# Sums of w_in moved to block 6, and another order of products, silus and sums in the last two blocks of a fused linear attention and MoE kernel

## Chip, cores and metric

The kernel runs on one core of one Trainium2 chip. The metric is the device time of one execution in microseconds (us), given as the median over runs of the same program; a profiled execution, one of its own, is where all views of the profile come from. TensorE is called PE here, VectorE DVE, ScalarE ACT, GpSimd POOL and SyncE SP, as in the profile.

## What is computed

The inputs are q, k and v of shape 8 x 8 x 576 x 64 (batch, heads, positions, head width), w_in (512 x 2048), w_out (2048 x 512) and beta (2048), all f32. The reference is a linear attention and then a layer with a gated activation:

```python
q_p, k_p = phi(q), phi(k)                      # elu(x) + 1
kv  = np.einsum('bhsd,bhse->bhde', k_p, v)
num = np.einsum('bhsd,bhde->bhse', q_p, kv)
den = np.einsum('bhsd,bhd->bhs', q_p, k_p.sum(2))[..., None] + 1e-06
x = (num / den).transpose(0, 2, 1, 3).reshape(4608, 512)
h = x @ w_in
g = h / (1 + np.exp(-beta * h))
return g @ w_out
```

## The kernel before

**Blocks.** The work goes by nine blocks of 512 tokens. Block b (0 to 7) holds 512 of the 576 positions of batch b; the 64 that are left over of each batch are gathered in a buffer `xT_tail` and make up block 8. Block 0 is written out by hand ahead of the loop; the loop `for b in range(1, B + 1)` (L1019, B = 8) does blocks 1 to 8. A block has two phases. In the first, H, PE computes h = x w_in, 16 tiles of 128 features by 512 tokens, and ACT writes silu(beta h) to SBUF as bf16 (`silu`, L409; w_out has been divided by beta before, which makes up for the factor). In the second, Y, PE computes g w_out, DVE and ACT add the parts, and SP stores the result.

**The order** of the work is written out by hand: each engine's queue runs in the order in which the program issues it, and an instruction that waits holds up those behind it on its engine. The attention of the following batches is put between as side work: `at(side, n, f)` says that f is issued at place n of a phase, `run(side, n)` issues it. In block 6 the H phase issues at place 1 the products k^T v of batch 7 (`kv_both`, evicted by DVE at L230 into `kv_q`), and at place 4 its numerators (`numer_all`: matmuls L332, DVE evictions L345 to L347, transposing DMAs L354).

**Fast products in Y.** `y_fast` does, in blocks 1 to 8, a 2 x 2 block product with 7 products in place of 8 (Strassen's in Winograd's form). It halves the tokens (columns 0:256 and 256:512 of g), the features (tiles 0 to 7 and 8 to 15) and the columns of w_out. It needs sums of w_out's blocks (`ws`, made once) and of g's blocks (`gs`, four buffers in `stage`, made by DVE in every block): `g_diff` (L723) makes gs[2]; `g_sums` (L730, L731) gs[0] and gs[1]; `g_last` (L726) gs[3] from gs[1]. Each is made in two calls of four tiles. The order on PE is ya (g plain), yd (gs[2]), ya again, yc (gs[1]), yb (gs[0]), yd again, yb again (gs[3]), 16 matmuls of 256 columns each (L951). Between them ACT copies ya (L967, L972) and DVE adds (L975 u2, L976 u3, L985, L988, L996). Block 8's yb goes in three parts (L923, L931), so that the last store is small.

**Fast products in H.** Blocks 1 to 6 use `h_phase`: sixteen plain tiles one after another. Blocks 7 and 8 use `h_fast`: eight tiles plain (4 to 7 and 12 to 15; `h_mm`, four matmuls of 512 columns, L401), and two groups of four (0 to 3 and 8 to 11) by the 2 x 2 scheme with 7 products of four matmuls of 256 columns each (`product`, L833). For this DVE makes sums of w_in (`h_w_sums(0)` and `h_w_sums(2)`, four subtractions or additions each, L785 to L788), which serve both blocks and lie in the buffer of v's f32 copy (`vf`, from which POOL's casts, L240, made `vaug`), and sums of x (`h_x_sums`, L807).

`products(fq)` gives the parts of one group. They use two two-bank PSUM tiles, `cw` (halves cw0 and cw1; the profile's `hc`) and `z` (one bank used; `hz`), and one bank z6 (also `hz`):

- `part1`: z6; DVE copies it to h_u[0] (L845). Then cw0 and z. DVE adds cw0 into h_u[0] (L852), and z and h_u[0] into h_u[1] (L853).
- `part2`: a product into cw1, one on top of cw0; DVE adds cw1 and h_u[1] into half of c2 (L858).
- `part3`: one product on top of z, one on top of cw1; DVE adds z and h_u[0] into the other half of c2 (L863) and h_u[0] into cw1 (L864).
- `out(0)`: two silus from cw. `out(1)`: two silus from c2 (L871).

The dependences are kept per tile, so the product into cw1 also waits for the addition L852, which reads cw0. PSUM banks come from a pool of four single banks (plain tiles, z6, ya to yb) and one of two double banks (cw and z).

Of the kernel before, what the change touches and what calls it, by code (L numbers as in the profile page):

```python
# [16 lines left out]
def kernel(  # L17
# [10 lines left out]
    nc = tc.nc  # L28

    B, H, S, D = q.shape  # L30
# [9 lines left out]
    HM = DM // 2  # L40
# [16 lines left out]
    def banks(name, shape=None, dt=F32):  # L57
# [13 lines left out]
    g_sb = [consts.tile([P, FC, 512], BF16, name=f"g{i}") for i in range(2)]  # L71
# [20 lines left out]
    gs = [  # L92
        st_b[:, n * 2048 : (n + 1) * 2048].rearrange("p (c t) -> p c t", c=8) for n in range(4)
    ]
# [189 lines left out]
    def rows_of(t):  # L284
        return P if t < NT - 1 else G
# [273 lines left out]
    for t in range(NT):  # L559
        n = rows_of(t)  # L560
# [157 lines left out]
    def at(side, n, *fs):  # L718
        side.setdefault(n, []).extend(fs)

    def g_diff(b, c):
        g = g_sb[b % 2]
        nc.vector.tensor_sub(gs[2][:, c], g[:, c, 0:HM], g[:, c, HM:512])  # L723

    def g_last(b, c):
        nc.vector.tensor_sub(gs[3][:, c], g_sb[b % 2][:, 8 + c.start : 8 + c.stop, 0:HM], gs[1][:, c])  # L726

    def g_sums(b, c0, c1, last=True):
        g, c, c2 = g_sb[b % 2], slice(c0, c1), slice(8 + c0, 8 + c1)
        nc.vector.tensor_add(gs[0][:, c], g[:, c, HM:512], g[:, c2, HM:512])  # L730
        nc.vector.tensor_sub(gs[1][:, c], gs[0][:, c], g[:, c, 0:HM])  # L731
        if last:
            g_last(b, c)

    def g_parts(b, ff):
        if ff in (3, 7):
# [4 lines left out]
    def h_phase(b, x, side):  # L741
# [31 lines left out]
    h_u = [  # L773
        xk[1].rearrange("p i j d -> p (i j d)").bitcast(F32)[:, n * 512 : (n + 1) * 512]
        for n in range(2)
    ]

    def h_w_plain(fq, f, r):

        return w_in_sb[fq][:, 2 * r : 2 * r + 2, f * 256 : (f + 1) * 256]  # L780

    def h_w_sums(fq):

        s, a = h_ws[fq // 2], lambda f, r: h_w_plain(fq, f, r)
        nc.vector.tensor_add(s[0], a(1, 0), a(1, 1))  # L785
        nc.vector.tensor_sub(s[1], s[0], a(0, 0))
        nc.vector.tensor_sub(s[2], a(0, 0), a(1, 0))
        nc.vector.tensor_sub(s[3], a(0, 1), s[1])  # L788

    def h_x_plain(b, r, t):  # L790

        if b == B:
            return xT_tail[:, :, 4 * t : 4 * t + 4, r]
        return xT[b % 2][:, :, 4 * t + r : 4 * t + 4 : 2]

    def h_x_sums(b):

        t = h_xs[b % 2]
        x = lambda r, t: h_x_plain(b, r, t)

        def like(a, c):
            return a.rearrange("p i (t n) -> p i t n", n=c.shape[-1])

        for k, (u, w) in enumerate((
            (x(0, 1), x(0, 0)), (x(1, 1), t[0]), (x(1, 1), x(0, 1)), (x(1, 0), t[1])
        )):
            nc.vector.tensor_sub(like(t[k], u), u, like(w, u) if k % 2 else w)  # L807

    def h_fast(b, x, side):
        run(side, 0)  # L810
        hps_of = {}

        def plain(ff):
            hps_of[ff] = bank("h_ps")
            h_mm(x, ff, hps_of[ff])

        def act(*ffs):
            for ff in ffs:
                silu(b, ff, hps_of[ff])

        def products(fq):
            s, t = h_ws[fq // 2], h_xs[b % 2]
            cw, z = banks("hc"), banks("hz")[:, 0]
            c2 = h_c2

            def product(ps, lhs, rhs, first):
                for a in range(2):
                    for i in range(2):
                        o = ps[:, a * 256 : (a + 1) * 256]
                        m = rhs[:, i]  # L830
                        if len(m.shape) > 2:
                            o = o.rearrange("p (t n) -> p t n", n=m.shape[-1])
                        nc.tensor.matmul(  # L833
                            o, lhs[:, i, a * P : (a + 1) * P], m,
                            start=(first and a == 0 and i == 0), stop=True,
                            skip_group_check=True,
                        )

            def w(f, r):
                return h_w_plain(fq, f, r)  # L840

            def part1():
                z6 = bank("hz")
                product(z6, s[1], t[1], True)
                nc.vector.tensor_copy(h_u[0], z6)  # L845

                for n in (1, 0) if fq == 0 else (0, 1):
                    if n:
                        product(cw[:, 0], w(0, 0), h_x_plain(b, 0, 0), True)
                    else:  # L850
                        product(z, s[2], t[2], True)
                nc.vector.tensor_add(h_u[0], cw[:, 0], h_u[0])  # L852
                nc.vector.tensor_add(h_u[1], z, h_u[0])  # L853

            def part2():
                product(cw[:, 1], s[0], t[0], True)
                product(cw[:, 0], w(0, 1), h_x_plain(b, 1, 0), False)
                nc.vector.tensor_add(c2[:, 1], cw[:, 1], h_u[1])  # L858

            def part3():  # L860
                product(z, w(1, 1), t[3], False)
                product(cw[:, 1], s[3], h_x_plain(b, 1, 1), False)
                nc.vector.tensor_add(c2[:, 0], z, h_u[0])  # L863
                nc.vector.tensor_add(cw[:, 1], cw[:, 1], h_u[0])  # L864

            def out(n):

                for a in range(2):
                    ff = 4 * fq + 2 * n + a
                    src = (cw, c2)[n][:, :, a * 256 : (a + 1) * 256]  # L870
                    nc.scalar.activation(  # L871
                        g_sb[b % 2][:, ff].rearrange("p (t n) -> p t n", t=2), src,
                        ACTF.Silu, scale=beta_c[:, ff : ff + 1],
                    )

            return part1, part2, part3, out

        p1, p2, p3, out = products(0)
        p1()
        plain(4)  # L880
        act(4)
        p2()
        plain(5)
        act(5)
        p3()
        plain(6)
        act(6)
        out(0)
        plain(7)
        act(7)  # L890
        out(1)
        plain(12)
        act(12)
        p1, p2, p3, out = products(2)
        p1()
        g_diff(b, slice(0, 4))
        plain(13)
        act(13)
        p2()
        plain(14)  # L900
        act(14)
        p3()
        out(1)
        g_diff(b, slice(4, 8))
        plain(15)
        act(15)
        out(0)
        g_sums(b, 4, 8)
        g_sums(b, 0, 4, last=False)

    def y_fast(b, side):

# [106 lines left out]
    for b in range(1, B + 1):  # L1019
        n, m = b + 1, b + 2  # L1020
        sh, sy = {}, {}
        if 2 <= b < B:
            at(sh, 0, lambda: tail_copy(b))
        if n < B:
            at(sh, 0, lambda: next_loads(n))
            at(sh, {1: 9, 2: 2}.get(b, 1), lambda: kv_both(n))
            at(sh, {1: 11, 2: 5}.get(b, 4), lambda: numer_all(n))
        if b == 1:
            at(sh, 4, lambda: w_sum(2))
            at(sh, 9, lambda: w_sum(1))  # L1030
            at(sy, 0, lambda: w_sum(3))
        if m < B:
            at(sy, 0, lambda: phi_tile(m, "q"), lambda: phi_tile(m, "k"))
            if b == 1:

                for pr in range(2):
                    at(sy, 0, lambda pr=pr: v_copy(nc.scalar, m, pr))
                for pr in range(2):
                    at(sy, 0, lambda pr=pr: phi_exp(m, "q", pr, xin(m, "q", pr)))
                    at(sy, 3 + pr, lambda pr=pr: phi_relu(m, "q", pr, xin(m, "q", pr)))  # L1040
                    at(sy, 3 + pr, lambda pr=pr: phi_min(m, "q", pr))
                at(sy, 4, lambda: q_trans_dma(m))
                at(sy, 5, lambda: phi_part(m, "k", 0))
                at(sy, 6, lambda: phi_part(m, "k", 1), lambda: table(ACTF.Silu))
            else:
                at(sy, 0, lambda: phi_part(m, "q", 0))
                at(sy, 1, lambda: phi_part(m, "q", 1))
                at(sy, 1, lambda: q_trans_dma(m))
                at(sy, 3, lambda: phi_part(m, "k", 0))
                at(sy, 4, lambda: phi_part(m, "k", 1), lambda: table(ACTF.Silu))  # L1050
        if b == B - 2:
            at(sy, 0, lambda: h_x_sums(B - 1), lambda: h_w_sums(0))
            at(sy, 6, lambda: h_w_sums(2))
        if b == B - 1:
            at(sy, 0, lambda: h_x_sums(B))
        if b >= B - 1:
            at(sy, 4, lambda: g_last(b, slice(0, 4)))
        (h_phase if b < B - 1 else h_fast)(b, xT[b % 2] if b < B else xT_tail, sh)
        y_fast(b, sy)

# [29 lines left out]
```

## Time and profile before

| | us |
|---|---|
| median of 3 runs | 276.71 (276.53 to 277.04) |
| the profiled execution's own time | 276.49 |
| its span, first to last instruction | 274.7 |
| block 6: H and Y on PE | 190.5 to 206.1, 206.1 to 218.3 |
| block 7: H and Y on PE | 218.3 to 233.1, 233.1 to 245.3 |
| block 8: H, then Y with the last stores | 245.3 to 258.5, 258.5 to 274.7 |

The profile is read in these views. The busy shares say for how much of the span each engine works. The chain that ended last goes back from the last instruction, at each step to what released it, and so names who set the end at every time. The timeline lists instructions in order of time, with the start, the length, the engine, the line and the tile; in square brackets stands how long the engine was idle before, and for whom. PEld is PE's loading of weights, which runs beside its matmuls; SPq and ACTq are DMAs that an engine issues. Starts of consecutive matmuls are more exact than their ends, which are modelled.

### The profile page before, as it was taken

To read this page: it belongs to the slowest core of one execution; us is meant where nothing else is said; L and a number is where in the kernel's file an instruction comes from. 1 tells how busy PE (TensorE), PEld (TensorE's weight loads), DVE (VectorE), ACT (ScalarE), POOL (GpSimd) and SP (SyncE) were. 2 spreads that over 40 slices of the span, in tenths; PEclk is the share of its full clock that TensorE was granted. 3 is DMA by queue.
4 is the path that set the end of the run, shared out by engine and by line. 5 is a ranking of instruction groups with operands and counts; after the bars stand their busy time and mean duration, and the time that the engine had idled before them with its cause. 6 is when DMAs were issued, how large, how long until landed. Compare 5 with 4: busy or idle time off the path is not lost.

```text
span 274.7 us, 6629 instructions
## 1 busy us (share of the span) xinstructions
PE 265.1 (96%) x2804; PEld 176.4 (64%) x2809; DVE 187.8 (68%) x362; ACT 170.8 (62%) x237; POOL 45.1 (16%) x64
## 2 busy tenths in 40 slices
PE   7899998999999999999999999999999979999994
PEld 2575454446865587458744875487548846886793
DVE  4871786899896776647766675668567577775754
ACT  4838877967776885689457945794572037406710
POOL 5922102043003403130303021300000000000000
PEclk9999999999999999999999999999999999999998
DMA  6999999658988996993699469955540140023013
GB/s 247 239 207 352 252 389 249 187 91 249 200 113 182 292 169 111 295 199 67 107 288 206 62 115 282 213 66 100 141 88 0 31 124 0 2 45 110 0 41 116
DMA packets 48958, 42.78 MB, mean 156 GB/s; under 512 B 30352, under 2 KB 40736, under 8 KB 48928
## 3 DMA queue, kind: packets, MB, share of 16 engines
q0 software_dynamic: 13040, 23.40, 36.7%
q1 hardware_dynamic: 35568, 18.75, 32.2%
q8 instruction: 22, 0.36, 0.5%
q10 hardware_dynamic: 320, 0.20, 0.2%
q14 instruction: 8, 0.07, 0.1%
HBM read 36.71 MB, written 9.44 MB: 168 GB/s over the span
## 4 chain that ended last, share of the span: by engine, by line
PE 82%; DMA 12%; DVE 3%; ACT 1%; issue 0%; POOL 0%; DVEq 0%
PE h_ps L401 36%; DMA vf<-in_v_dram 10%; PE yd L951 10%; PE ya L951 10%; PE yb L951 9%; PE yc L951 5%; PE hc L833 3%; PE kvp L222 2%; PE nps L332 2%; PE hz L833 2%; DMA stage<-in_q_dram 1%; PE yb L923 1%; PE y_ps L416 1%; PE xtp L381 1%; PE nps L297 1%; DVE xs_sb L310 1%
## 5 line engine op out<-in xcount | busy, mean ns | idle before, releaser
L409 ACT ACTIVATE g<-h_ps,beta_c 128x512 bf16<-128x512 f32 x128 | 86.3, 688 | 66.3 <-PE h_ps L401 66.3
L401 PE MATMUL h_ps<-xT,w_in 128*128 128x512 bf16 (+1 forms) x528 | 108.5, 360 | 0.1
L401 PEld LDWEIGHTS <-w_in 128*128 128x128 bf16 x560 | 51.1, 98 | 52.6 <-DMA xT<-xs_sb 0.3
L951 PEld LDWEIGHTS <-stage 128*128 128x128 bf16 x480 | 46.9, 98 | 5.7 <-issue 0.2
L951 PEld LDWEIGHTS <-g 128*128 128x128 bf16 x384 | 37.5, 98 | 6.0
L951 PE MATMUL ya<-w_out,g 128*128 128x256 bf16 x256 | 30.6, 273 | 0.0
L730 DVE TENSOR_TENSOR stage<-g 128x1024 bf16<-128x1024 bf16 x16 | 11.0, 689 | 15.3 <-ACT g L409 15.3
L240 POOL CAST vaug<-vf 128x1152 bf16<-128x1152 f32 x11 | 14.6, 1351 | 37.2 <-DMA vf<-in_v_dram 37.2
L347 DVE TENSOR_TENSOR xs_sb<-nps,rden 128x448 bf16<-128x448 f32 (+2 forms) x24 | 18.2, 758 | 0.8
L723 DVE TENSOR_TENSOR stage<-g 128x1024 bf16<-128x1024 bf16 x16 | 11.9, 742 | 9.4 <-ACT g L409 9.4
L162 ACT ACTIVATE e<-xk 128x1152 bf16<-128x1152 bf16 (+1 forms) x15 | 16.7, 1159 | 2.5 <-DMA xk<-in_k_dram 2.5
L162 ACT ACTIVATE e<-xq 128x1152 bf16<-128x1152 bf16 x14 | 15.6, 1159 | 1.7 <-DMA xq<-in_q_dram 1.7
L155 ACT ACT_TABLE_LOAD x12 | 15.4, 1283 | 0.2
L951 PE MATMUL yd<-ws,stage 128*128 128x256 bf16 x128 | 15.3, 273 | 0.0
L951 PE MATMUL yc<-ws,stage 128*128 128x256 bf16 x128 | 15.3, 273 | 0.0
L951 PE MATMUL yd<-ws,g 128*128 128x256 bf16 x128 | 15.3, 273 | 0.0
L416 PE MATMUL y_ps<-w_out,g 128*128 128x512 bf16 x60 | 14.6, 379 | 0.3 <-issue 0.2
L174 DVE TENSOR_TENSOR phi_q<-e,r 128x1152 bf16<-128x1152 bf16 x16 | 12.3, 772 | 3.4 <-ACT e L162 2.3
L367 POOL COPY xT_tail<-xT 128x256 bf16<-128x256 bf16 x6 | 2.7, 456 | 68.1 <-DMA xT<-xs_sb 68.1
L174 DVE TENSOR_TENSOR phi_k<-e,r 128x1152 bf16<-128x1152 bf16 x16 | 12.9, 809 | 1.4
L951 PE MATMUL yb<-ws,stage 128*128 128x256 bf16 x112 | 13.4, 273 | 0.0
L951 PE MATMUL yb<-w_out,stage 128*128 128x256 bf16 x112 | 13.4, 272 | 0.0
(126 smaller groups left out, 302.0 us busy)
## 6 DMA issues: line engine op xcount, KB each, us to landing
vf<-in_v_dram POOLq DMA_DIRECT2D x7, 1152.0 KB, 8.5
out_dram<-y SPq DMA_DIRECT2D x29, 256.0 KB, 4.0
xq<-in_q_dram POOLq DMA_DIRECT2D x7, 576.0 KB, 12.1
xk<-in_k_dram POOLq DMA_DIRECT2D x7, 576.0 KB, 15.2
w_in<-in_moe_w_in_dram POOLq DMA_DIRECT2D x4, 512.0 KB, 11.4
g<-in_moe_w_out_dram POOLq DMA_DIRECT2D x2, 1024.0 KB, 17.6
stage<-in_moe_w_out_dram POOLq DMA_DIRECT2D x2, 1024.0 KB, 21.9
stage<-in_q_dram SPq DMA_DIRECT2D x2, 576.0 KB, 4.3
```

What stands on the lines that cost most here:

```text
L155: nc.scalar.activation(act0, warm[:, 0:1], func)
L162: nc.scalar.activation(e, x, ACTF.Exp)
L174: nc.vector.tensor_tensor(st[b, a][:, pr].rearrange("p j (h d) -> p j h d", h=2), st[b, a, pr, "e"].rearrange("p h j d -> p j h d"), st[b, ...
L240: eng.tensor_copy(dst, src)
L347: nc.vector.tensor_mul(xs_sb[:, ils, v0 * D : v1 * D].rearrange("p i (u d) -> p i u d", d=D), pv[:, :, :, 0:D], rden[:, :, :, None].to_bro ...
L401: nc.tensor.matmul(hp[:, c0:c1].rearrange("p (t n) -> p t n", n=n), w_in_sb[ff // 4][:, kc, (ff % 4) * P : (ff % 4 + 1) * P], xm, start=(k ...
L409: nc.scalar.activation(g_sb[b % 2][:, ff, :], hp, ACTF.Silu, scale=beta_c[:, ff : ff + 1])
L416: nc.tensor.matmul(yp[:, c0:c1], g_sb[b % 2][:, ff, t * P : (t + 1) * P], w_out_sb[i][:, c, c0:c1], start=(ff == 0), stop=(ff == FC - 1), ...
L723: nc.vector.tensor_sub(gs[2][:, c], g[:, c, 0:HM], g[:, c, HM:512])
L730: nc.vector.tensor_add(gs[0][:, c], g[:, c, HM:512], g[:, c2, HM:512])
L833: nc.tensor.matmul(o, lhs[:, i, a * P : (a + 1) * P], m, start=(first and a == 0 and i == 0), stop=True, skip_group_check=True,)
L951: nc.tensor.matmul(ps[:, p * HM : (p + 1) * HM], lhs(c, p), rhs(c), start=(first and p == 0 and c == 0), stop=True, skip_group_check=True,)
```

## The change

h_w_sums(0) and h_w_sums(2) move from the Y phase of block 6 (places 0 and 6) to its H phase (places 0 and 2). In `part1` the product cw0 always comes ahead of z (before, this held for the first group alone). In `part3` the product on cw1 comes ahead of the one on z, and the addition into cw1 ahead of the one into c2. In `h_fast` tile 4 is issued first, ahead of the first `part1`, so that `part2` of the first group stands behind tile 5 and `part3` behind tile 6. Of the second group, `out(0)` comes ahead of `out(1)` and in two halves, around tile 15; the second g_diff is issued ahead of tile 14. gs[3] of the first four tiles (L726 by `g_last`) is made with the other g sums ahead of Y, and no longer behind the first yb.

```diff
-    def g_last(b, c):
-        nc.vector.tensor_sub(gs[3][:, c], g_sb[b % 2][:, 8 + c.start : 8 + c.stop, 0:HM], gs[1][:, c])
-
-    def g_sums(b, c0, c1, last=True):
+    def g_sums(b, c0, c1):
         g, c, c2 = g_sb[b % 2], slice(c0, c1), slice(8 + c0, 8 + c1)
         nc.vector.tensor_add(gs[0][:, c], g[:, c, HM:512], g[:, c2, HM:512])
         nc.vector.tensor_sub(gs[1][:, c], gs[0][:, c], g[:, c, 0:HM])
-        if last:
-            g_last(b, c)
+        nc.vector.tensor_sub(gs[3][:, c], g[:, c2, 0:HM], gs[1][:, c])
...
                 nc.vector.tensor_copy(h_u[0], z6)
-
-                for n in (1, 0) if fq == 0 else (0, 1):
-                    if n:
-                        product(cw[:, 0], w(0, 0), h_x_plain(b, 0, 0), True)
-                    else:
-                        product(z, s[2], t[2], True)
+                product(cw[:, 0], w(0, 0), h_x_plain(b, 0, 0), True)
+                product(z, s[2], t[2], True)
...
             def part3():
+                product(cw[:, 1], s[3], h_x_plain(b, 1, 1), False)
                 product(z, w(1, 1), t[3], False)
-                product(cw[:, 1], s[3], h_x_plain(b, 1, 1), False)
+                nc.vector.tensor_add(cw[:, 1], cw[:, 1], h_u[0])
                 nc.vector.tensor_add(c2[:, 0], z, h_u[0])
-                nc.vector.tensor_add(cw[:, 1], cw[:, 1], h_u[0])
-
-            def out(n):
-
-                for a in range(2):
+
+            def out(n, parts=range(2)):
+
+                for a in parts:
...
+        plain(4)
+        act(4)
         p1, p2, p3, out = products(0)
         p1()
-        plain(4)
-        act(4)
-        p2()
         plain(5)
         act(5)
-        p3()
+        p2()
         plain(6)
         act(6)
+        p3()
         out(0)
         plain(7)
         act(7)
...
         p2()
+        g_diff(b, slice(4, 8))
         plain(14)
         act(14)
         p3()
-        out(1)
-        g_diff(b, slice(4, 8))
+        out(0, [0])
         plain(15)
         act(15)
-        out(0)
+        out(0, [1])
+        out(1)
         g_sums(b, 4, 8)
-        g_sums(b, 0, 4, last=False)
+        g_sums(b, 0, 4)
...
         if b == B - 2:
-            at(sy, 0, lambda: h_x_sums(B - 1), lambda: h_w_sums(0))
-            at(sy, 6, lambda: h_w_sums(2))
+            at(sh, 0, lambda: h_w_sums(0))
+            at(sh, 2, lambda: h_w_sums(2))
+            at(sy, 0, lambda: h_x_sums(B - 1))
         if b == B - 1:
             at(sy, 0, lambda: h_x_sums(B))
-        if b >= B - 1:
-            at(sy, 4, lambda: g_last(b, slice(0, 4)))
```

## The prediction

> **What bounds the kernel now.** I read the busy shares first, then the chain that ended last, then the timeline where the chain leaves TensorE.
>
> ```profile
> PE 265.1 (96%) x2804; PEld 176.4 (64%) x2809; DVE 187.8 (68%) x362; ACT 170.8 (62%) x237; POOL 45.1 (16%) x64
> ```
>
> TensorE (PE) is busy nearly throughout, so only a stretch in which PE stands still can be won without removing matmuls, and the change removes none. In its last 70 us the chain leaves PE once, at the start of block 7:
>
> ```profile
> 216.76 1.76 PE yb L951 x16
> 218.52 0.02 issue
> 218.54 0.69 DVE y L996
> 219.24 0.34 DVE vf L785
> ...
> 220.70 0.61 DVE xk L845
> 221.31 0.03 issue
> 221.34 0.02 DVEq L852
> 221.36 0.04 issue
> 221.40 0.70 DVE xk L852
> 222.10 0.04 issue
> 222.15 1.03 PE hc L833 x8
> ```
>
> The columns are start, length, engine, line. VectorE (DVE) evicts the last y of block 6 (L996), makes four w_in sums (L785 to L788), and only then copies the first product out (L845) and adds to it (L852), for which `part2` waits. The timeline shows the same on PE:
>
> ```profile
> 219.65 1.03 PE L401 MATMUL h_ps<-xT,w_in 128*128 128x512 bf16 x4
> 220.62 0.68 DVE L845 COPY xk<-hz 128x512 f32<-128x512 f32 x1
> 221.40 0.69 DVE L852 TENSOR_TENSOR xk<-hc,xk 128x512 f32<-128x512 f32 x1
> 222.15 0.60 PE L833 MATMUL hc<-xq,vf 128*128 128x256 bf16 x4 [1.47 <-DVE xk L852]
> 222.20 0.69 DVE L853 TENSOR_TENSOR xk<-hz,xk 128x512 f32<-128x512 f32 x1
> ```
>
> Block 8 has no w_in sums and is the comparison; its timeline has this, and later the wait for the last g sum:
>
> ```profile
> 246.10 0.68 DVE L845 COPY xk<-hz 128x512 f32<-128x512 f32 x1
> 247.63 0.60 PE L833 MATMUL hc<-xq,vf 128*128 128x256 bf16 x4
> 268.40 0.68 DVE L726 TENSOR_TENSOR stage<-g,stage 128x1024 bf16<-128x1024 bf16 x1
> 269.13 1.77 PEld L923 LDWEIGHTS <-stage 128*128 128x128 bf16 x24 [0.20 <-DVE stage L726]
> ```
>
> **Units, all from rows.** A plain tile is 0.863 us of PE (three take 2.59 in the chain), a product 0.437 (0.44 for four matmuls). From the end of a product to the DVE instruction that reads it: 0.20 (second z6 of block 8: start 252.82, end 253.26, L845 at 253.46). From DVE to the waiting matmul 0.05 (222.10 to 222.15), to ScalarE (ACT) 0.03. An f32 DVE eviction lasts 0.69; the next may start 0.60 after it if independent (229.58, 230.19, 230.78) and 0.78 to 0.80 after it if it reads its result (220.62, 221.40, 222.20). ACT silus in a row start 0.57 to 0.62 apart. Eight tiles and fourteen products are 13.02 us of PE. From the first matmul of H to the first of y, block 7 took 218.34 to 233.06 = 14.72, so 1.70 of standstill; block 8 245.29 to 258.55 = 13.26, so 0.24. These are the prizes.
>
> **w_in's sums into block 6.** Four sums take 1.55 from first start to last end (219.15 to 220.70). In block 6 the DVE is free from 191.39 (L996 of block 5 ends) to 193.29 (the kv_q cast), and from 193.72 to 195.81 (first g difference). The first four run from about 191.3 to 192.9, the others from 193.7 to 195.2: both fit, by 0.4 and 0.6. What they overwrite is v's f32 copy, last read by GpSimd's casts, which end at 174.9, 16 us before. Queued behind them is the kv_q cast, for which the numerators' matmuls wait at 195.84; the cast ends at 193.72, so 2.1 us of delay would still be hidden. Cost nothing; with all cover gone, at most 3.1. Neither set issues a DMA; as built, the queues of SP and GpSimd keep their order. In block 6's y nothing gets earlier: u2 at 213.38 waited for PE.
>
> **Block 7's H, step by step.** Its start, 218.34, stays: PE runs without a gap through block 6. All starts:
> - Tile 4 218.34, z6 219.20, cw0 219.64, z 220.08, tile 5 220.51 to 221.37.
> - DVE: L996 may be followed at 219.15; z6 ended at 219.64, so the copy starts at 219.84, L852's add 220.62, ending 221.31. `part2` may start at 221.36; PE comes at 221.37. The 1.47 is gone, by a margin of 0.01. Cover is cw0, z and a tile, 1.74, against 0.20 + 0.78 + 0.69 + 0.05 = 1.72.
> - cw1 221.37, cw0 again 221.81 to 222.25, tile 6 to 223.11. The add to c2 (old L858) runs 222.45 to 223.14. Before, `part3` opened with z, which does not wait for it; now it opens with cw1, which does: 223.19. **Gap 0.08.** z follows to 224.07.
> - Tiles 7 and 12 to 225.79, z6 to 226.23, cw0 to 226.67, z to 227.10, tile 13 to 227.96. cw0 and z take over buffers freed at 225.12 (DVE) and 225.8 (ACT's second silu of out(0)): no wait. Copy 226.43, adds 227.21 (ends 227.90) and 228.01; `part2` at 227.96.
> - cw1 and cw0 end at 228.83, tile 14 at 229.69. On the DVE the first g difference still stands ahead of the c2 add: 228.62, so the add runs 229.21 to 229.90, and cw1 starts at 229.95, not 229.69. **Gap 0.26.** z and tile 15 end at 231.69, where y starts. The second g difference, now ahead of `part3`'s adds, runs 229.82 to 230.50, while they wait for cw1 until 230.59: hidden, by 0.09.
> - PSUM banks are free in time: the last of y's by L996 at 219.23, for tile 6 at 222.25.
>
> So block 7 takes 13.35 (13.02 + 0.34) instead of 14.72: **-1.37**. Block 8 has the same instructions in the same order, so 13.35 instead of 13.26: **+0.09**, what the new order costs where there were no sums to move.
>
> **Trailing edges.** Silus (with part 3's adds at 230.59 and 231.19): out(0)a 231.31, tile 15 231.92, out(0)b 232.49, out(1) 233.06 to 234.37, copy of ya to 234.8; the second ya needs both at 235.19: hidden by 0.4. The g sums follow at 232.65, 233.38, 234.11, then 234.72, 235.43 (ending 236.12), 236.16; yc needs the fifth at 236.94. The cover shrinks nowhere: before, the fifth ended at 238.10 with yc at 238.31. The sixth, formerly L726 behind yb, now ends at 236.85; block 8's x sums follow to 238.3, under u2 at 238.96. In block 8 it no longer holds the last product: yd ends at 269.05, the product started at 269.14: **-0.09**.
>
> Sum: -1.37 + 0.09 - 0.09 = **-1.37**. The profiled execution took 276.49 (span 274.7), so 275.12. The median of the runs is 276.71, 0.22 above it; I forecast on the median: **275.3**.
>
> **Bounds of what the trace does not show.** No row has cw1 first in `part3`, nor a g difference ahead of an add that PE awaits at once. Least: all DVE pairs follow at the independent 0.60. Then the c2 add waits only for its product (229.03) and the second gap is 0.08: 0.18 less per block, in all -1.73. Most: nothing overlaps and a g difference ends before the add starts (229.40): gap 0.45, 0.19 more per block, -0.99. I take the middle, since both pitches are in rows of these very lines. With the 0.22 between execution and median: 274.98 to 275.72.
>
> The Trainium skill (VectorE: DVE Perf Modes, The DRAIN you can't avoid) says that a semaphore between two Vector instructions "costs nothing extra". The rows above disagree: 0.78 to 0.80 with one, 0.60 without. By the page the sum would be the least case, -1.73; the measurement decides.
>
> **Rivals.**
> 1. *The order of the products costs more than it seems.* `part2` has 0.01 to spare in each half, and `part3` now waits for the add made last. If each of the four hand-overs per block is 0.1 late on top, that is 0.8 over both blocks: -0.57, 276.1. For: the margins. Against: each term is a row of this trace. 0.10.
> 2. *Slower: the g difference blocks the DVE.* It waits for ACT's out(1) of tiles 2 and 3, which stands behind tile 7's silu, and the add for which PE now waits at once is queued behind it. By my times out(1) ends at 227.7, 0.9 before the g difference could start. Each us beyond that slack is paid in both blocks: slower than before once ACT is 0.9 + 0.69 = 1.6 late, nearly three silus. One us beyond the slack: -1.37 + 2.0, 277.3. Against: that slack. 0.03.
> 3. *The change does not take the stall away*: the first copy still comes late, because the y eviction ahead of it does, or the sums outgrow their free time in block 6. Then about 276.7. Against: block 8, with the same eviction and no sums, lost 0.24. 0.04.
>
> **Numbers.** The forecast has 0.83, rival 1 0.10, 2 0.03, 3 0.04. The range goes from the least case less the runs' spread of about 0.2 to the most case plus it: 274.8 to 275.9. Rivals lie outside with 0.17. What a measurement here tells from no change is about 0.2%, 0.55 us, so faster means below 276.16: the forecast and most of rival 1, 0.92; within 0.05; slower 0.03.
>
> **What will show it.** Right: no PE wait for the add of `part1` above 0.1 in block 7; a PE wait of 0.2 to 0.4 before the last cw1 of both blocks and 0.1 before the earlier one; H of 13.2 to 13.6 us in both blocks; w_in's sums at 191 to 195 with block 6 as long as before; no PE wait in the last product. Wrong: H of block 7 over 14, block 8 longer by over 0.4, or any new wait of PE in block 6.

## The result and the profile after

The changed kernel takes 275.50 us (median of 22 runs, 274.61 to 277.11), against 276.67 before (22 runs beside them, 275.97 to 278.75). The ratio is 0.9947, with a 95% interval of 0.9929 to 0.9965, or 1.47 us less (1.0 to 2.0). The medians themselves differ by 1.17; the means, 277.01 and 275.54, by 1.47, since five of the runs before took over 278. The prediction was 275.3 and a gain of 1.37.

The profiled execution took 275.76 us, only 0.73 less than the one before. It had reached block 6 half a us later (first matmul at 191.00 instead of 190.50), after work that is the same in both kernels; this is most of what is missing from the 1.35 below. Of the half us, 0.28 is already there when the load of v for block 1 lands. In the chain that ended last this is one piece in each kernel (start, length), before:

```profile
18.67 22.11 DMA vf<-in_v_dram
```

and after:

```profile
19.41 21.65 DMA vf<-in_v_dram
```

So the two traces are compared from a common point: from the first matmul of block 6's H to the last addition on DVE. Before that is 190.50 to 271.11, or 80.61; after, 191.00 to 270.26, or 79.26: **1.35 less.** The granted TensorE clock is 1.00 from 190 to 270 in both, so it is no part of the difference.

The timeline of the changed kernel at the start of block 7, beside the lines that the prediction showed of before:

```profile
218.85 1.03 PE L401 MATMUL h_ps<-xT,w_in 128*128 128x512 bf16 x4
...
220.35 0.69 DVE L841 COPY xk<-hz 128x512 f32<-128x512 f32 x1 [0.61 <-PE hz L829]
...
221.14 0.69 DVE L844 TENSOR_TENSOR xk<-hc,xk 128x512 f32<-128x512 f32 x1
...
221.89 0.60 PE L829 MATMUL hc<-xq,vf 128*128 128x256 bf16 x4
```

The copy of z6 (L841, before L845) starts 1.50 after H's first matmul, not 2.28; `part2`'s matmul follows tile 5 without a wait (tile 5 starts at 221.02, and 0.863 later is 221.88). The wait of 1.47 for L852 is gone, and the chain that ended last stays on PE here. Two smaller waits have come in its place, both ahead of `part3`'s product on cw1:

```profile
222.76 1.03 PE L401 MATMUL h_ps<-xT,w_in 128*128 128x512 bf16 x4
222.96 0.69 DVE L850 TENSOR_TENSOR xk<-hc,xk 128x512 f32<-128x512 f32 x1 [0.33 <-PE hc L829]
...
223.70 0.60 PE L829 MATMUL hc<-xT,vf 128*128 128x256 bf16 x4
...
226.94 0.69 DVE L841 COPY xk<-hz 128x512 f32<-128x512 f32 x1 [1.31 <-PE hz L829]
...
227.74 0.69 DVE L844 TENSOR_TENSOR xk<-hc,xk 128x512 f32<-128x512 f32 x1
...
228.53 0.69 DVE L845 TENSOR_TENSOR xk<-hz,xk 128x512 f32<-128x512 f32 x1
...
229.14 0.68 DVE L723 TENSOR_TENSOR stage<-g 128x1024 bf16<-128x1024 bf16 x1
...
229.35 1.03 PE L401 MATMUL h_ps<-xT,w_in 128*128 128x512 bf16 x4
229.74 0.69 DVE L850 TENSOR_TENSOR xk<-hc,xk 128x512 f32<-128x512 f32 x1
...
230.48 0.60 PE L829 MATMUL hc<-xT,vf 128*128 128x256 bf16 x4
...
232.21 1.91 PE L944 MATMUL ya<-w_out,g 128*128 128x256 bf16 x16
```

At the first of the two, tile 6 ends at 222.76 + 0.863 = 223.62, the add into c2 (L850) at 223.65, the product starts at 223.70, 0.08 late. At the second, tile 14 ends at 230.21, L850 only at 230.43, and the product starts at 230.48, 0.27 late. This is where the chain now leaves PE, in both blocks.

Ahead of the second gap the DVE works without a break from the copy of z6 on: 0.20 after z6 (which ends at 226.74), then 0.80, 0.79, 0.61 and 0.60 from start to start, the add's 0.69 and 0.05 to PE are 3.74, while PE has four products and two tiles to do, 3.47. The g difference (L723), which went ahead of L850, is one of the five.

H of block 7 runs from 218.85 to 232.21, 13.36; block 8's from 244.44 to 257.79, 13.35, with gaps of 0.08 and 0.26. In block 8 before, PE stood instead ahead of each `part2`: 0.17 (tile 4 ends at 247.46, the product starts at 247.63) and 0.08, by H's length 0.24 in all. So the new order trades 0.24 for 0.34.

At the end the product of gs[3] follows yd at once (16 matmuls, 1.75), where it waited for L726 before (yd at 267.30, the product at 269.14):

```profile
266.55 1.91 PE L944 MATMUL yd<-ws,g 128*128 128x256 bf16 x16
...
268.29 1.93 PE L916 MATMUL yb<-w_out,stage 128*128 128x256 bf16 x24
```

Block 6's H takes what was moved there. DVE's timeline:

```profile
191.20 0.69 DVE L989 TENSOR_TENSOR y<-yb,u 128x512 f32<-128x512 f32 x1 [0.17 <-PE yb L944]
191.81 0.41 DVE L781 TENSOR_TENSOR vf<-w_in 128x512 bf16<-128x512 bf16 x1
...
193.79 0.43 DVE L230 CAST kv_q<-kvp 128x260 bf16<-128x260 f32 x1 [0.43 <-PE kvp L222]
194.13 0.42 DVE L781 TENSOR_TENSOR vf<-w_in 128x512 bf16<-128x512 bf16 x1
...
196.31 0.69 DVE L723 TENSOR_TENSOR stage<-g 128x1024 bf16<-128x1024 bf16 x1 [0.63 <-ACT g L409]
```

The sums (L781 to L784) fill the time between the y eviction and the kv_q cast, and between the cast and the g difference. The cast stands where it stood, 2.79 after the phase's first matmul (before 193.29 - 190.50 = 2.79), and H and Y of block 6 take as long as before: H 206.62 - 191.00 = 15.62, before 206.12 - 190.50 = 15.62; Y 12.23, before 12.22.

### The profile page after: what moved, and what is told of

The parts are those of the page before. It is cut to its first block, busy times and chain, and to the rows that moved or that the text cites. A ratio compares the mean times of both kernels' runs of the same rounds, so it can differ in the third digit from the quotient of the medians.

```text
span 274.0 us, 6637 instructions
## 1 busy us (share of the span) xinstructions
PE 266.0 (97%) x2809; PEld 176.6 (64%) x2809; DVE 187.8 (69%) x362; ACT 171.3 (63%) x237; POOL 45.8 (17%) x64
## 4 chain that ended last, share of the span: by engine, by line
PE 79%; DMA 13%; DVE 3%; POOL 1%; issue 1%; ACT 0%; DVEq 0%; POOLq 0%
PE h_ps L401 35%; PE ya L944 10%; PE yd L944 10%; PE yb L944 9%; DMA vf<-in_v_dram 8%; PE yc L944 5%; DMA w_in<-in_moe_w_in_dram 4%; PE kvp L222 2%; PE hc L829 2%; PE nps L332 2%; PE hz L829 2%; DMA stage<-in_q_dram 1%; PE yb L916 1%; PE y_ps L416 1%; POOL vf L99 1%
## 5 line engine op out<-in xcount | busy, mean ns | idle before, releaser
L727 DVE TENSOR_TENSOR stage<-g 128x1024 bf16<-128x1024 bf16 x16 | 11.2, 697 | 16.3 <-ACT g L409 16.3
L240 POOL CAST vaug<-vf 128x1152 bf16<-128x1152 f32 x11 | 13.9, 1293 | 41.0 <-DMA vf<-in_v_dram 27.9
L723 DVE TENSOR_TENSOR stage<-g 128x1024 bf16<-128x1024 bf16 x16 | 12.1, 758 | 8.1 <-ACT g L409 8.1
L367 POOL COPY xT_tail<-xT 128x256 bf16<-128x256 bf16 x6 | 3.6, 608 | 64.5 <-DMA xT<-xs_sb 64.5
L944 PE MATMUL yb<-ws,stage 128*128 128x256 bf16 x112 | 13.4, 273 | 0.0
L944 PE MATMUL yb<-w_out,stage 128*128 128x256 bf16 x112 | 13.4, 272 | 0.0
```

The costliest lines, as they stand in the source:

```text
L240: eng.tensor_copy(dst, src)
L944: nc.tensor.matmul(ps[:, p * HM : (p + 1) * HM], lhs(c, p), rhs(c), start=(first and p == 0 and c == 0), stop=True, skip_group_check=True,)
```

## The experiments

My theory was that the DVE queue alone made the stall: the second four sums stood between the last y eviction and the copy of z6. The standstill there is 1.64: tile 4 ends at 219.65 + 0.863 = 220.51, and `part2` starts at 222.15 (the 1.47 in the profile's brackets counts from the modelled end). The rival was that the new order, tile 4 ahead of `part1`, is what hides it. All kernels compute the whole result. The order of the silus and the place of the second g difference were not run alone. Since the time of one execution moves by more than most of these effects, the table gives the parts that the trace shows: H of blocks 7 and 8 (first matmul to the first of y), and the way from block 6's first matmul to the last addition on DVE.

| kernel | H of 7 | H of 8 | block 6 to end | change | ratio to before (95%) |
|---|---|---|---|---|---|
| before | 14.72 | 13.26 | 80.61 | | |
| changed | 13.36 | 13.35 | 79.26 | -1.35 | 0.9947 (0.9929 to 0.9965) |
| changed, again | 13.36 | 13.36 | 79.26 | -1.35 | 0.9946 (0.9925 to 0.9967) |
| sums only | 13.26 | 13.26 | 79.15 | -1.46 | 0.9927 (0.9902 to 0.9953) |
| second sums only | 13.26 | 13.26 | 79.16 | -1.45 | 0.9956 (0.9935 to 0.9977) |
| order only | 14.11 | 13.36 | 80.02 | -0.59 | 0.9965 (0.9939 to 0.9990) |
| last sum early | 14.73 | 13.26 | 80.52 | -0.09 | 1.0004 (0.9988 to 1.0020) |
| z first | 13.02 | 13.02 | 78.59 | -2.02 | 0.9915 (0.9887 to 0.9944) |
| z first, again | 13.02 | 13.02 | 78.59 | -2.02 | 0.9927 (0.9900 to 0.9954) |
| difference behind the add | 13.24 | 13.23 | 79.32 | -1.29 | 0.9938 (0.9917 to 0.9959) |
| all sums at place 0 | 13.36 | 13.36 | 79.27 | -1.34 | 0.9966 (0.9952 to 0.9979) |

### The sums alone

```diff
--- before
-            at(sy, 0, lambda: h_x_sums(B - 1), lambda: h_w_sums(0))
-            at(sy, 6, lambda: h_w_sums(2))
+            at(sh, 0, lambda: h_w_sums(0))
+            at(sh, 2, lambda: h_w_sums(2))
+            at(sy, 0, lambda: h_x_sums(B - 1))
```

> The kernel before with one part of the change: w_in's sums move to block 6's H, and nothing else. My theory (the eight DVE sums behind the last y eviction are the whole stall): block 7's H becomes like block 8's, 13.26 us instead of 14.72, with PE waits of 0.16 for part1's add and 0.08 later; block 8's H stays 13.26 and the last product keeps its wait of 0.09. Sum -1.46, a ratio of 0.9947. Rival (tile 4 ahead of part1 is what hides the stall, the sums being short): block 7's H stays above 14 and the time within 0.3 us of before.

Its timeline at the start of block 7:

```profile
219.71 0.68 DVE L845 COPY xk<-hz 128x512 f32<-128x512 f32 x1
...
220.50 0.69 DVE L852 TENSOR_TENSOR xk<-hc,xk 128x512 f32<-128x512 f32 x1
...
221.24 0.60 PE L833 MATMUL hc<-xq,vf 128*128 128x256 bf16 x4
```

The y eviction starts at 219.10, the copy 0.61 after it, and the matmul waits 0.17 (tile 4 ended at 221.07). H of block 7 is 13.26, as block 8's: -1.46. The theory's number came; the rival's did not. The expectation named all eight sums; only four of them stood behind the last y eviction (L785 to L788 at 219.15 to 220.70 in the kernel before), and a later run takes those alone. This kernel is not behind the whole change but 0.11 ahead of it in the trace, 0.10 in H of block 7 and 0.09 in that of block 8, less 0.09 at the end (the last g sum, which this kernel leaves where it was).

### The order alone

```diff
--- changed
-            at(sh, 0, lambda: h_w_sums(0))
-            at(sh, 2, lambda: h_w_sums(2))
-            at(sy, 0, lambda: h_x_sums(B - 1))
+            at(sy, 0, lambda: h_x_sums(B - 1), lambda: h_w_sums(0))
+            at(sy, 6, lambda: h_w_sums(2))
```

> The changed kernel with w_in's sums put back into block 6's Y. My theory: the second four sums still hold the copy of z6 to 2.28 us after H begins, the add ends at 3.75, and tile 5 covers only a part: PE waits 0.77 in block 7 for part1's add, then 0.08 and 0.26; H of block 7 14.13, of block 8 13.35, no wait in the last product. Sum -0.59 + 0.09 - 0.09 = -0.59, a ratio of 0.9979. Rival (the order does the work): H of block 7 13.4 and the time as in the changed kernel, 0.995.

Its timeline at the start of block 7:

```profile
219.89 0.68 DVE L841 COPY xk<-hz 128x512 f32<-128x512 f32 x1
...
220.67 0.69 DVE L844 TENSOR_TENSOR xk<-hc,xk 128x512 f32<-128x512 f32 x1
...
221.42 0.60 PE L829 MATMUL hc<-xq,vf 128*128 128x256 bf16 x4 [0.60 <-DVE xk L844]
```

The sums end at 219.97, the copy starts 2.27 after H's first matmul, and PE waits 0.77 after tile 5 (which ended at 220.65). Tile 4 in front gives 0.87 of cover and no more. With the gaps of `part3`, H of block 7 comes to 14.11, 0.61 less than before; block 8's is 0.10 longer and the end 0.09 shorter, in all the -0.59 that was written. The timing (0.9965) has the rival's 0.995 in its interval too; H of 14.11, where the rival asked for 13.4, decides. So order and sums are two ways to the same 1.64: where the sums are gone, the order has nothing left to hide, and its own price shows.

### Only the second four sums

```diff
--- before
-            at(sy, 0, lambda: h_x_sums(B - 1), lambda: h_w_sums(0))
-            at(sy, 6, lambda: h_w_sums(2))
+            at(sh, 2, lambda: h_w_sums(2))
+            at(sy, 0, lambda: h_x_sums(B - 1), lambda: h_w_sums(0))
```

> The kernel before, with only the second four sums (tiles 8 to 11) moved to block 6's H; the first four stay in block 6's Y at place 0. My theory: the first four ran from 210.6 to 212.1, and the next DVE work, u2, waited for PE until 213.4, so they cost nothing where they were; the result is as with all eight moved: block 7's H 13.26, sum -1.46, ratio 0.9947. Rival (both groups cost their share): about half, H 14.0, ratio 0.9975.

DVE's timeline in Y of block 6:

```profile
211.28 0.42 DVE L788 TENSOR_TENSOR vf<-w_in,vf 128x512 bf16<-128x512 bf16 x1
212.96 0.69 DVE L975 TENSOR_TENSOR u<-yc,r 128x512 f32<-128x512 f32 x1 [1.26 <-PE yc L951]
```

The first four end at 211.70 and u2 (L975) waits for PE until 212.96, as before; at the seam the eviction starts at 218.13 and the copy at 218.74. -1.45, the same as with all eight: the first four cost nothing where they were, and all of the gain is in the four that stood at the seam between two blocks. The timing (0.9956) has both the theory's 0.9947 and the rival's 0.9975 in its interval; the trace decides.

### The last g sum alone

```diff
--- before
-        g_sums(b, 0, 4, last=False)
+        g_sums(b, 0, 4)
...
-        if b >= B - 1:
-            at(sy, 4, lambda: g_last(b, slice(0, 4)))
```

> The kernel before, with gs[3] of the first four tiles made with the other g sums ahead of Y, and nothing else. My theory: the wait of PE before block 8's last product (0.09) goes and nothing else moves: H of block 7 14.72 and of block 8 13.26, sum -0.09, ratio 0.9997, which the timing cannot tell from 1; the trace decides. Rival (the added 0.61 us ahead of x's sums in block 7's Y makes u2 late, and with it the second yd): a new PE wait of 0.1 to 0.5 there, 240 to 243 us into the span, ratio 1.000 to 1.002.

At the end of its timeline:

```profile
269.21 1.91 PE L951 MATMUL yd<-ws,g 128*128 128x256 bf16 x16
...
270.95 1.93 PE L923 MATMUL yb<-w_out,stage 128*128 128x256 bf16 x24
```

The last product starts 1.74 after yd, the length of its 16 matmuls: the gap before it is gone, no new one came, and the way to the end is 0.09 shorter; the timing can't see it. The stall in block 7 stays as it was, 1.64, and u2 in Y of block 7 is not late: no wait of PE shows there.

### The product on z first

```diff
--- changed
             def part3():
-                product(cw[:, 1], s[3], h_x_plain(b, 1, 1), False)
                 product(z, w(1, 1), t[3], False)
-                nc.vector.tensor_add(cw[:, 1], cw[:, 1], h_u[0])
+                product(cw[:, 1], s[3], h_x_plain(b, 1, 1), False)
                 nc.vector.tensor_add(c2[:, 0], z, h_u[0])
+                nc.vector.tensor_add(cw[:, 1], cw[:, 1], h_u[0])
...
         p3()
-        out(0, [0])
+        out(1)
         plain(15)
         act(15)
-        out(0, [1])
-        out(1)
+        out(0)
```

> The changed kernel, with part3 in the old order (the product on z ahead of the one on cw1, the add into c2 first) and the second group's out(1), tile 15, out(0) as before. My theory: z waits only for an add that ended 0.9 us earlier, and its 0.44 covers the c2 add, so both gaps (0.08 and 0.27 in each block) vanish: H 13.02 to 13.05 in both blocks, 0.3 less than in the changed kernel in each; yc's fifth g sum then ends only some 0.06 before it is needed, so up to 0.1 may come back in Y. Against the kernel before -1.9 to -2.0, a ratio of 0.993. Rival (the gaps come from the cw buffer or from ScalarE, not from the order of the two products): H stays at 13.35, ratio 0.995.

The edit also puts the second group's silus back as they were. They stand behind `part3` in the program, and the first group's gap goes too, where only the order in `part3` was changed. The timeline ahead of the last two products of block 7:

```profile
229.29 0.68 DVE L850 TENSOR_TENSOR xk<-hc,xk 128x512 f32<-128x512 f32 x1
...
229.77 0.60 PE L829 MATMUL hz<-xq,w_in 128*128 128x256 bf16 x4
...
230.20 0.60 PE L829 MATMUL hc<-xT,vf 128*128 128x256 bf16 x4
```

The product on z starts at 229.77, when tile 14 ends, and its 0.44 covers the add (L850 ends at 229.97). No PE gap is left in either H: 13.02, the sum of the matmuls. What was feared in Y did not come: the fifth g sum (L728) ends at 236.62, yc starts at 236.74, without a wait. It is 0.67 shorter than the changed kernel in the trace, and of the kernels tried it is the fastest: 274.74 us (6 runs), ratio 0.9915 (0.9887 to 0.9944). Run again in the same rounds as the changed kernel, on another occasion:

> The changed kernel once more, on the same chip and in the same rounds as the next kernel. My theory: from the first matmul of block 6's H to the last DVE instruction 79.3 us, against 80.6 before; ratio to before 0.995.

> The version with part3 in the old order once more, beside the changed kernel. My theory: it keeps H at 13.02 in both blocks and 78.6 us from the first matmul of block 6's H to the last DVE instruction, 0.67 less than the changed kernel; ratio to before 0.9925. Rival (its lead over the changed kernel lay in the runs, not in the order): both ratios alike.

Both traces repeat to 0.01 (79.26 and 78.59). In the timing it is 275.19 (12 runs) against 274.64 (7 runs), with ratios to before whose intervals overlap: 0.9946 (0.9925 to 0.9967) and 0.9927 (0.9900 to 0.9954). The lead of 0.67 is shown by the traces; the timing only points the same way.

### The g difference behind the add

```diff
--- changed
         p1()
-        g_diff(b, slice(0, 4))
         plain(13)
         act(13)
         p2()
+        g_diff(b, slice(0, 4))
         g_diff(b, slice(4, 8))
```

> The changed kernel, with the first g difference issued behind part2's add into c2 instead of ahead of it, just ahead of the second. My theory (DVE start pitch: the difference takes 0.60 on the queue, and the add behind it is what PE waits for): the add starts when its product is done, the second gap falls from 0.27 to 0.08; H 13.18 in both blocks. The part3 add into cw1 moves behind two differences, 0.25 later, which can bring back up to 0.1 in Y behind ScalarE. Sum against the changed kernel -0.15 to -0.35, a ratio to before of 0.994. Rival (the pitch does not matter, the gap is the hand-over between the engines): the gap stays 0.27.

Its timeline at the same place, and at the second ya of block 7:

```profile
229.33 0.69 DVE L850 TENSOR_TENSOR xk<-hc,xk 128x512 f32<-128x512 f32 x1 [0.39 <-PE hc L829]
...
230.07 0.60 PE L829 MATMUL hc<-xT,vf 128*128 128x256 bf16 x4
...
234.82 0.59 ACT L960 COPY r<-ya 128x512 f32<-128x512 f32 x1
...
235.46 1.25 PE L944 MATMUL ya<-w_out,g 128*128 128x256 bf16 x10
```

Half a miss. The gap falls from 0.27 to 0.14, not to 0.08: the add starts 0.25 after its product's modelled end (229.08), where the first group's starts 0.20 after. Where the 0.05 comes from I can't say. And what was won in H is lost in Y: the add into cw1 stands behind two differences, ScalarE's silus and its copy of ya slip, and the second ya, which needs that copy (234.82 to 235.41), starts 0.16 late. The sum is +0.06 against the changed kernel, where -0.15 to -0.35 was expected; I had put what comes back at up to 0.1. That the difference ahead of the add makes 0.13 of the second gap's 0.27 is borne out; that taking it away pays is not.

### All sums ahead of the cast

```diff
--- changed
-            at(sh, 0, lambda: h_w_sums(0))
-            at(sh, 2, lambda: h_w_sums(2))
+            at(sh, 0, lambda: h_w_sums(0), lambda: h_w_sums(2))
```

> The changed kernel, with all eight sums at place 0 of block 6's H, ahead of the kv_q cast. It measures the cover there. My theory: the sums run about 3.0 us, until 1.0 after the cast could have started; the cast ends 2.1 us before the numerators' matmuls need it, so PE does not wait and block 6's H keeps 15.6 us; time as the changed kernel, ratio 0.995. Rival (the side work of block 6 is tight): PE waits up to 1.0 before the numerators, ratio 0.998.

DVE's timeline in block 6:

```profile
194.80 0.42 DVE L230 CAST kv_q<-kvp 128x260 bf16<-128x260 f32 x1
```

The cast starts 1.0 later than in the changed kernel (3.74 after the phase's first matmul, not 2.79). The numerators' matmuls start 5.36 after the phase's first matmul here and 5.35 in the changed kernel, and H takes 15.63 against 15.62. So of the cover of 2.1 us that the prediction counted on, 1.0 was used up and cost nothing; the rest was not tried. The way to the end, 79.27, is the changed kernel's; the timing, 0.9966 (0.9952 to 0.9979), lies between the 0.995 of the theory and the 0.998 of the rival and excludes both by a little, so the reading rests on the trace.

## Why the prediction was right, step by step

- **The stall and its cause.** The prediction put the wait for L852 down to four sums on DVE (1.64 of its 1.70 of standstill in block 7). Moving just those gives -1.45, to what block 8 has. Right.
- **Block 6 for nothing.** H of block 6 is unchanged at 15.62, the cast starts at the same place, and even a delay of 1.0 costs nothing. Right. The sums were put at 191.3 to 192.9 and 193.7 to 195.2, on the time axis of before; shifted by 0.50, they run 191.81 to 193.36 and 194.13 to 195.68.
- **Block 7's H, 13.35.** Measured 13.36; the `part2` wait with 0.01 to spare did not open. The two new gaps, forecast at 0.08 and 0.26, are 0.08 and 0.27.
- **Block 8's H, 13.35, so +0.09.** Measured 13.35. The new order costs by itself 0.09 to 0.10 per block, as the kernel with the sums alone confirms from the other side.
- **The end, -0.09.** The wait is gone; the kernel with this part alone gives -0.09.
- **The bounds.** Both pitches of DVE came as in the rows of before: 0.60 from the g difference to the independent add (229.14, 229.74), 0.79 between a copy and the add that reads its result (220.35, 221.14). The sum by the Trainium skill's sentence that the semaphore costs nothing extra (VectorE: DVE Perf Modes, The DRAIN you can't avoid) would have left gaps of 0.08; the second was 0.27. The page's sentence comes from a row of copies, which no run here repeats; in the rows here the pairs at 0.78 to 0.80 are those in which the second instruction reads what the first wrote.
- **The rivals.** None came. The first, a 0.1 more at each hand-over: hand-overs were as in the rows. The second, DVE blocked by a g difference that waits for ScalarE: in block 7 out(1) ended at 228.14 and the difference started at 229.14, a slack of 1.0 where 0.9 was reckoned. No run made ScalarE late on purpose, so its price was not tried. The third, that the stall stays: gone.
- **Y of block 7, nothing.** The silus and g sums in their new order were to be hidden. Y takes 12.23 in both kernels (before 233.06 to 245.29, after 232.21 to 244.44).
- **The sum.** -1.37 forecast, -1.35 in the traces and -1.47 (1.0 to 2.0) in the timing. 275.3 forecast, 275.50 measured; single executions differ by more than that through their start alone: block 6 began between 189.77 and 192.40 in the eleven profiled executions, of kernels that do the same work until there.

What the prediction did not say is that the change could have been better. It priced the gaps of `part3`'s new order at 0.34 per block and left it there; had it asked what a product that needs no late add would do in its place, it would have found the 0.67 that z first brings. That product was in its place before: the harm is in this one part of the new order, and the rest of it does good (79.15 with the sums alone, 78.59 with z first).

## What to carry to other kernels

At a seam between two stages look at what stands in the queue of the engine that evicts: work of no urgency issued there delays the first eviction of the next stage, and here the matmul engine paid for it nearly in full (the copy came 2.28 after H's first matmul with the sums ahead of it and 0.81 without; PE lost 1.45), while the same work in a gap of the previous stage was free (block 6's H 15.62 with it and without). Price a move and a new order apart, against the same stall: here the order alone (with the last g sum's 0.09) was worth 0.59, the sums alone 1.46, and both 1.35, since the order by itself costs 0.1 per block once the stall is gone. When a product must wait for an addition on another engine, put the product that doesn't wait ahead of it, and count the hand-overs (here 0.20 to the evicting engine, 0.69 for the addition, 0.05 back) against the matmuls in between.

## What the runs showed of the hardware that was not expected

- A DVE instruction that reads the result of the one before it starts 0.73 after it when that is its only wait (the g sums L727 to L728 of the changed kernel, 233.14 to 233.87; in f32 u2 to u3 of before, 240.32 to 241.05) and 0.78 to 0.80 when it also waits for PE. Such a pair has a semaphore instruction of its own ahead of the second (in the changed kernel L844 has four for four additions, 21 ns each, L728 one for sixteen); that this makes the difference of 0.06 is likely, but no run took it away. Independent ones start 0.60 apart (229.14 and 229.74).
- The parts of a trace that don't depend on loads repeat to 0.01 us: 79.26 twice and 78.59 twice, on executions that reached block 6 0.1 and 0.9 apart. Differences of 0.09 that 12 runs can't time are plain there.
